# Scores of the first two batches as 64 by 64 corner matmuls, with q stored without zero blocks

## The chip, the cores and the metric

The kernel runs on one core of a Trainium2 chip. Five engines work side by side, each through its own queue in order: TensorE (PE; its weight loads are listed apart as PEld), VectorE (DVE), ScalarE (ACT), GpSimd (POOL) and SyncE (SP), which here only issues DMA transfers. The metric is the device time of one execution in microseconds (us); the median of several runs is compared.

## The reference

Windowed attention over 8 batches, 8 heads, 576 tokens and a head dimension of 64, followed by a feed-forward block with a low-rank mix over tokens. Four heads see a plain window of 32 tokens, four a dilated one.

```python
scores = scale * np.matmul(q, k.transpose(0, 1, 3, 2))
mask_plain = (rel >= 0) & (rel < window)                                   # window = 32
mask_dil = (rel >= 0) & (rel < window * dilation) & (rel % dilation == 0)  # dilation = 4
scores = np.where(masks[None, :, :, :], scores, -1000000000.0)
attn = np.exp(scores - np.max(scores, axis=-1, keepdims=True))
attn = attn / (np.sum(attn, axis=-1, keepdims=True) + 1e-09)
x = np.matmul(attn, v)                 # heads side by side: 576 x 512 a batch
u = x + (x.transpose(0, 2, 1) @ U @ V).transpose(0, 2, 1)
out = u + np.maximum(u @ w_ch1, 0.0) @ w_ch2
```

## The kernel before

**Units and groups.** Tokens of the dilated heads are put in another order by the host, so that their window too is 32 neighbouring tokens. A unit is a pair of heads and a block of 64 queries (`QB`); it needs 96 keys (`KB`: the block and the 32 ahead of it). Four units form a group, nine groups a batch. For a unit the host stores q and k transposed, both heads one above the other on 128 partitions (64 numbers a head). In batches 0 and 1 q of head 0 has its own 64 columns and zeros in the other 64, and q of head 1 the reverse, so that a single float32 matmul of 128 rows by 128 columns against the 96 columns of k gives the scores of both heads, 128 queries by 96 keys (line 388). That makes a row of `QK1` = 128 + 96 = 224 numbers.

**Three ways to load and score.** In batch 0 (groups 0 to 8) `load_qk` brings a whole group at once (line 304), and nine such loads, each followed by a load of v (line 313), are the first things on SP's queue; the loads of the masks, the identity, and then U (`ut`), V (`vt`) and the feed-forward weights come between and behind. In batch 1 `fetch` brings two units at a time (line 336). From batch 2 on, eight of the nine groups of a batch are wide: two neighbouring query blocks of one head fill the 128 columns, without zeros, and the score matmul is that of line 377 on operands split into a high and a low part. The ninth group (`ODD`, the fifth of a batch) has no partner block and stays in the form of batches 0 and 1: four units a batch, one load each (line 342), 24 units in all.

**After the scores.** VectorE adds the mask and takes the minimum of the scaled scores (lines 405 and 408), ScalarE takes the exponential (line 412), the result is transposed by TensorE (line 425) or VectorE (lines 438 and 441), and line 451 multiplies with v: two matmuls a unit, one for each head, each in one half of the array's columns. VectorE divides by the sums (lines 455, 456, 481). The low-rank mix follows (lines 499 to 547).

**The feed-forward block.** Twelve chunks of 384 tokens. For each of the 16 blocks of hidden features `layer1` runs 12 matmuls (line 766), ScalarE and VectorE split the result (lines 771 and 772), and `layer2` runs 9 matmuls into three accumulators (line 786). The weights are loaded as 64-bit floats and narrowed on the chip (lines 201 to 226) during batch 0 and chunk 0.

**What sets the order.** Batch 0 comes first, with the weights' steps put between. Then the chunks run, and `slot` takes attention work of the batches ahead from a list that is sorted by due times, some after every fourth matmul of line 766 and after every third of line 786. So the attention of batch 1 lies in chunk 0 (four units at a time, `step = UNITS`), and from batch 2 on `STEP` = 1: a unit's scores stand alone between feed-forward matmuls. A scheduler then settles each engine's order of instructions by a simulated timeline.

Of the kernel before, what the change touches and what calls it, by code (L numbers as in the profile page):

```python
# [26 lines left out]
P = 128  # L27
QB = 64
NJ = S // QB
KB = QB + WIN  # L30
# [8 lines left out]
CTOK = CT * P  # L39
NCHUNK = NTILE // CT  # L40
UNITS = 4
QK1 = P + KB
DV = D + 1
PV = 2 * DV
KW = P + WIN
# [69 lines left out]
def mask_of(off, n):  # L115
    i = np.arange(n)[:, None]
    c = np.arange(n + WIN)[None, :] - WIN
    ok = (i - c >= 0) & (i - c < WIN)
    if off is not None:
        ok &= (i >= off) == (c >= off)  # L120
    return np.where(ok, 0.0, NEG).astype(np.float32)


def token_of(half, s):
    return s if half == 0 else DIL * (s % RES) + s // RES
# [27 lines left out]
def attention_moe_kernel(ctx: ExitStack, tc: tile.TileContext, qk1, qk2, vv, masks, wide, ident, ut, vt, w1, w2, out):  # L153
    nc = tc.nc
# [110 lines left out]
    at = {}  # L265
# [35 lines left out]
    def load_qk(g):  # L301
        if (g, 0) not in loaded:
            t = early.tile([P, UNITS, QK1], F32, tag="qk", name=f"qk{g}", bufs=QKS)
            nc.sync.dma_start(out=t, in_=qk1[g])
# [22 lines left out]
    def is_odd(n):  # L327
        return n // UNITS % NGB == ODD

    def fetch(n):  # L330
        if n >= UNITS * NG or n in raws:
            return
        if n < N2:
            if n % 2 == 0:
                raw = work.tile([P, 2, QK1], F32, tag="qks", name=f"qkr{n}", bufs=TB)
                nc.sync.dma_start(out=raw, in_=qk1[n // UNITS][:, n % UNITS:n % UNITS + 2])
                raws[n] = raw[:, 0]
                raws[n + 1] = raw[:, 1]
        else:
            raw = work.tile([P, QK2], F32, tag="qk", name=f"qkr{n}", bufs=QKB)  # L340
            m = QK1 if is_odd(n) else QK2
            nc.sync.dma_start(out=raw[:, 0:m], in_=qk2[n - N2][:, 0:m])
            raws[n] = raw

    def split_qk(n):
        if n < N2 or n >= UNITS * NG or n in pairs:
            return
        fetch(n)
        raw = raws[n]
        if is_odd(n):  # L350
            return
        t = work.tile([P, QK3], F32R, tag="qks", name=f"qks{n}", bufs=TB)
        nc.scalar.copy(out=t[:, 0:QK2], in_=raw)  # L353
        nc.gpsimd.tensor_tensor(out=t[:, QK2:], in0=raw[:, P:], in1=t[:, P:QK2].bitcast(F32), op=ALU.subtract)  # L354
        lo = slice(D, P)
        eng = nc.vector if Q_DVE else nc.gpsimd
        eng.tensor_tensor(out=t[lo, 0:P], in0=raw[lo, 0:P], in1=t[lo, 0:P].bitcast(F32), op=ALU.subtract)  # L357
        pairs[n] = t
# [6 lines left out]
    def score(g, u):  # L365
        n = UNITS * g + u
        two = n >= N2 and not is_odd(n)
        if u == 0:
            p_sb = work.tile([P, UNITS, KW], F32, tag="p", name=f"p{g}", bufs=2)
            pool, n_ = (early, 3) if g < NGB else (work, 2)  # L370
            nmax = pool.tile([P, UNITS], F32, tag="nmax", name=f"nmax{g}", bufs=n_)
            state[g] = [p_sb, nmax, None]
        if two:
            sp = psum.tile([P, 2 * KW], F32, tag="ps", name=f"s{g}_{u}")
            split_qk(n)
            t = pairs.pop(n)
            nc.tensor.matmul(sp, lhsT=t[:, 0:P], rhs=t[:, P:], start=True, stop=True)  # L377
        else:
            if n >= N2:
                sp = psum.tile([P, 1, KB], F32, tag="ps", name=f"s{g}_{u}")  # L380
            elif u == 0:
                sp = psum.tile([P, UNITS, KB], F32, tag="acc" if g < NGB else "ps", name=f"s{g}", bufs=3)
            else:
                sp = state[g][2]
            if g >= NE:
                fetch(n)
            t = raws[n] if g >= NE else loaded[g, 0][:, u]
            nc.tensor.matmul(sp[:, u % sp.shape[1], :], lhsT=t[:, 0:P], rhs=t[:, P:QK1], start=True, stop=True)  # L388
        state[g][2] = state[g, u] = sp

    def soften(g, u):
# [214 lines left out]
    def batch_items(b):  # L606
# [3 lines left out]
        for s in range(NGB + LAG):  # L610
# [16 lines left out]
            def some(us, g=g):  # L627
                for u in us:
                    score(g, u)
                for u in us:  # L630
                    n = UNITS * g + u
                    if n >= N2:
                        split_qk(n + LOOK)
                        fetch(n + LOOK + DMA_LOOK)
                    elif n >= UNITS * NE and n % 2 and n + 2 * TB - 1 < N2:
                        fetch(n + 2 * TB - 1)
                for u in us:
                    soften(g, u)
# [109 lines left out]
    for c in range(NCHUNK):  # L748
# [59 lines left out]
        for i in range(CT):  # L808
            t = c * CT + i
# [5 lines left out]
def lay_out(q, k, v, U, V, w1, w2):  # L815

    f = np.float32
    qk1 = np.zeros((B, len(TILES), 2, P, QK1), f)
    qk2 = np.zeros((B - SPLIT, NGB, UNITS, P, QK2), f)
    vv = np.ones((B, len(TILES), 2, KB, PV), f)  # L820
    for half in range(2):
        perm = np.array([token_of(half, s) for s in range(S)])
        hs = slice(half * HH, (half + 1) * HH)
        qp = q[:, hs][:, :, perm].reshape(B, 2, 2, S, D)
        kp = np.zeros((B, 2, 2, WIN + S, D), f)
        vp = np.zeros((B, 2, 2, WIN + S, D), f)
        kp[..., WIN:, :] = k[:, hs][:, :, perm].reshape(B, 2, 2, S, D)
        vp[..., WIN:, :] = v[:, hs][:, :, perm].reshape(B, 2, 2, S, D)
        for j in range(NJ):
            at = TILES.index((half, j))  # L830
            ks = slice(QB * j, QB * j + KB)
            for h in range(2):
                hr = slice(h * D, (h + 1) * D)
                qk1[:, at, :, hr, h * QB:(h + 1) * QB] = qp[:, :, h, QB * j:QB * (j + 1)].transpose(0, 1, 3, 2)
                qk1[:, at, :, hr, P:] = kp[:, :, h, ks].transpose(0, 1, 3, 2)
                vv[:, at, :, :, h * DV:h * DV + D] = vp[:, :, h, ks]
        for i in range(NJ // 2):
            g = TILES.index((half, 2 * i)) // 2
            for u in range(UNITS):
                for r in (slice(0, D), slice(D, P)):  # L840
                    qk2[:, g, u, r, :P] = qp[SPLIT:, u // 2, u % 2, P * i:P * (i + 1)].transpose(0, 2, 1)
                    qk2[:, g, u, r, P:] = kp[SPLIT:, u // 2, u % 2, P * i:P * i + KW].transpose(0, 2, 1)
    qk1 = qk1.reshape(B, NGB, UNITS, P, QK1)
    qk2[:, ODD, :, :, :QK1] = qk1[SPLIT:, ODD]
    qk2 = qk2.reshape((B - SPLIT) * NGB * UNITS, P, QK2)
    qk1 = np.ascontiguousarray(qk1[:SPLIT].reshape(SPLIT * NGB, UNITS, P, QK1).transpose(0, 2, 1, 3))
    vv = np.ascontiguousarray(vv.reshape(B * NGB, UNITS, KB, PV).transpose(0, 2, 1, 3))

    masks = np.stack([np.tile(mask_of(off, QB), (2, 1)) for off in MASK_AT], axis=1)
    wide = np.stack([mask_of(off, P) for off in WIDE_AT], axis=1).astype(ml_dtypes.bfloat16)  # L850

    raw = np.int64
    U, V, w1, w2 = (np.ascontiguousarray(x).view(raw) for x in (U, V, w1, w2))
    ut = np.zeros((P, NU, RANK), raw)
    for a in range(4):
        ut[:, a] = U[a * P:(a + 1) * P]
        ut[:, 4 + a] = U[64 + a * P:64 + (a + 1) * P]
    ut[0:64, 8] = U[512:576]
    ut[64:128, 8] = U[0:64]
    perm = np.array([token_of(1, s) for s in range(S)])  # L860
    for p, js in enumerate(DPART):
        ut[:QB * len(js), 9 + p] = U[perm[QB * js[0]:QB * (js[-1] + 1)]]
    vt = np.zeros((4, RANK, P + S), raw)
    vt[:, :, 64:64 + S] = V
    return {
        "qk1": qk1,
        "qk2": qk2,
        "vv": vv,
        "masks": masks,
        "wide": wide,  # L870
        "ident": np.eye(P, dtype=f),
        "ut": ut.reshape(P, NU * RANK),
        "vt": vt.reshape(P, P + S),
        "w1": w1,
        "w2": w2,
    }
# [15 lines left out]
```

## Time and profile before

| what | value |
|---|---|
| median of 3 runs | 1024.16 us (1022.04 to 1024.59) |
| profiled execution | 1024.88 us, its span 1023.1 us |
| granted TensorE clock, mean | 0.980 |
| PE busy | 983.6 us (96%) |
| DVE, ACT, POOL busy | 624.1, 410.0, 327.9 us |
| DMA | 103.34 MB, 101 GB/s over the span |
| matmuls of line 388 | 192 (two for each of 96 units) |

In rows of the profile, `out<-in` names the tiles written and read, `128*128 128x96` gives the rows and columns of the array that a matmul uses and then the shape of its output, and `x8` counts instructions. `s` is the tile of scores, `qk` and `qkr` the loaded q and k, `pv` the result of line 451, `ph` and `acc` those of lines 766 and 786, `raw` a loaded piece of a weight. [...]

### The profile page before, as it was taken

What the parts mean: (1) busy time and instruction counts of PE and PEld (TensorE: products, weight loads), DVE (VectorE), ACT (ScalarE), POOL (GpSimd) and SP (SyncE); (2) the same over time, 40 slices, a digit from 0 to 9 for tenths busy, and PEclk for the clock granted to TensorE, in tenths of its full rate; (3) what the DMA queues carried; (4) which work ended last, traced back from release to release, by engine and by line L of the source; (5) the groups of instructions that cost most, each with busy time, mean ns of one, the idle gap of its engine ahead of it and who ended that gap; (6) DMA issues with size and microseconds to landing.
All of it is one profiled execution on the core that took longest, in us unless ns stands there. A gap on an engine that the chain in (4) does not pass through costs nothing.

```text
span 1023.1 us, 18253 instructions
## 1 busy us (share of the span) xinstructions
PE 983.6 (96%) x5928; PEld 863.6 (84%) x5928; DVE 624.1 (61%) x2149; ACT 410.0 (40%) x985; POOL 327.9 (32%) x520
## 2 busy tenths in 40 slices
PE   7589998999999999999999999999999999999998
PEld 6388776888888889898888888788888888899996
DVE  4878876777368755777557873787647864411211
ACT  5889873343244423445233432434323442111110
POOL 0568863252143421344131621425213431000000
PEclk9679997999999999999999999999999999999999
DMA  9687643243323423333242432434332420500000
GB/s 255 201 271 234 190 136 106 62 134 87 93 81 83 119 73 90 103 109 100 65 111 74 127 87 52 133 81 121 94 80 81 120 63 25 134 1 1 32 1 32
DMA packets 96912, 103.34 MB, mean 101 GB/s; under 512 B 12816, under 2 KB 83536, under 8 KB 96816
## 3 DMA queue, kind: packets, MB, share of 16 engines
q1 hardware_dynamic: 96816, 102.16, 35.4%
q8 instruction: 48, 0.79, 0.3%
q14 instruction: 48, 0.39, 0.1%
HBM read 80.08 MB, written 17.30 MB: 95 GB/s over the span
## 4 chain that ended last, share of the span: by engine, by line
PE 86%; DMA 5%; DVE 3%; ACT 3%; POOL 1%; issue 1%; SPq 1%; DVEq 0%; POOLq 0%; ACTq 0%
PE acc L786 38%; PE ph L766 37%; PE pv L451 3%; PE s L377 3%; PE t L521 2%; PE m L545 1%; DMA raw<-ut 1%; DMA qk<-qk 1%; PE s L388 1%; DMA qkr<-qk 1%; POOL v L219 1%; ACT v L210 1%; ACT sign L211 1%; DMA raw<-w 1%; DMA v<-vv 1%
## 5 line engine op out<-in xcount | busy, mean ns | idle before, releaser
L786 PE MATMUL acc<-w2h,hh 128*128 128x512 f32 x576 | 229.5, 398 | 1.6 <-DVE x L811 1.1
L786 PE MATMUL acc<-w2l,hh 128*128 128x512 f32 x576 | 228.8, 397 | 0.0
L354 POOL TENSOR_TENSOR qks<-qkr,qks 128x160 fp32r<-128x160 f32 x192 | 103.5, 539 | 385.1 <-ACT qks L353 254.3
L772 DVE SCALAR_TENSOR_TENSOR hl<-ph,hh 128x384 fp32r<-128x384 f32 x192 | 106.2, 554 | 180.4 <-ACT hh L771 179.1
L786 PE MATMUL acc<-w2h,hl 128*128 128x512 f32 x576 | 212.5, 399 | 0.0
L771 ACT ACTIVATE hh<-ph 128x384 fp32r<-128x384 f32 x192 | 93.4, 487 | 268.7 <-PE ph L766 244.1
L766 PE MATMUL ph<-uth,w1l 128*128 128x384 f32 x768 | 175.1, 340 | 0.0
L766 PE MATMUL ph<-utl,w1h 128*128 128x384 f32 x768 | 173.0, 339 | 1.2 <-DVE utl L604 1.2
L766 PE MATMUL ph<-uth,w1h 128*128 128x384 f32 x768 | 172.5, 340 | 0.6 <-ACT uth L603 0.3
L412 ACT ACTIVATE p<-p,nmax 128x160 f32<-128x160 f32 (+1 forms) x288 | 111.0, 408 | 123.5 <-DVE nmax L408 122.5
L766 PEld LDWEIGHTS ph<-uth,w1h 128*128 128x128 f32 x768 | 138.6, 189 | 17.1 <-ACT uth L603 1.7
L766 PEld LDWEIGHTS ph<-utl,w1h 128*128 128x128 f32 x768 | 135.0, 188 | 2.9 <-DVE utl L604 1.6
L766 PEld LDWEIGHTS ph<-uth,w1l 128*128 128x128 f32 x768 | 136.2, 189 | 1.1 <-issue 0.4
L353 ACT CAST qks<-qkr 128x288 fp32r<-128x288 f32 x192 | 80.7, 429 | 125.1 <-PE s L377 92.8
L786 PEld LDWEIGHTS acc<-w2h,hl 128*128 128x128 f32 x576 | 107.7, 189 | 23.8 <-issue 0.4
L786 PEld LDWEIGHTS acc<-w2h,hh 128*128 128x128 f32 x576 | 108.5, 188 | 18.5 <-ACT hh L771 2.2
L786 PEld LDWEIGHTS acc<-w2l,hh 128*128 128x128 f32 x576 | 108.5, 188 | 15.9
L438 DVE STREAM_TRANSPOSE pt<-p 32x128 f32<-32x128 f32 x384 | 115.7, 301 | 10.1 <-ACT p L412 5.1
L405 DVE TENSOR_TENSOR p<-s,wide_sb 128x160 f32<-128x160 f32 x192 | 60.2, 319 | 74.1 <-PE s L377 72.3
L357 POOL TENSOR_TENSOR qks<-qkr,qks 64x128 fp32r<-64x128 f32 x192 | 90.6, 472 | 15.1
L501 POOL TENSOR_TENSOR xhl<-x,xhl 128x256 fp32r<-128x256 f32 (+1 forms) x68 | 50.1, 758 | 80.3 <-ACT xhl L499 48.9
L377 PE MATMUL s<-qks 128*128 128x320 f32 x192 | 60.8, 325 | 1.7 <-DVE x L547 1.7
(75 smaller groups left out, 977.2 us busy)
## 6 DMA issues: line engine op xcount, KB each, us to landing
qkr<-qk SPq DMA_DIRECT2D x192, 144.0 KB, 2.2
raw<-w SPq DMA_DIRECT2D x26, 512.0 KB, 5.0
v<-vv SPq DMA_DIRECT2D x126, 97.5 KB, 2.1
out<-x SPq DMA_DIRECT2D x36, 256.0 KB, 2.2
zd<-z SPq DMA_DIRECT2D x120, 64.0 KB, 2.0
xt<-zd SPq DMA_DIRECT2D x30, 256.0 KB, 2.9
qk<-qk SPq DMA_DIRECT2D x9, 448.0 KB, 9.4
qkr<-qk SPq DMA_DIRECT2D x18, 224.0 KB, 4.4
```

What stands on the lines that cost most here:

```text
L353: nc.scalar.copy(out=t[:, 0:QK2], in_=raw)
L354: nc.gpsimd.tensor_tensor(out=t[:, QK2:], in0=raw[:, P:], in1=t[:, P:QK2].bitcast(F32), op=ALU.subtract)
L357: eng.tensor_tensor(out=t[lo, 0:P], in0=raw[lo, 0:P], in1=t[lo, 0:P].bitcast(F32), op=ALU.subtract)
L377: nc.tensor.matmul(sp, lhsT=t[:, 0:P], rhs=t[:, P:], start=True, stop=True)
L405: nc.vector.tensor_tensor(out=p_sb[:, u, :], in0=sp[:, 0:KW], in1=wide_sb[:, kind], op=ALU.add)
L412: nc.scalar.activation(out=p_sb[:, u, 0:w], in_=p_sb[:, u, 0:w], func=AF.Exp, bias=nmax[:, u:u + 1], scale=-1.0,)
L438: nc.vector.transpose(out=to[:, :, WIN * (r % 2):WIN * (r % 2 + 1)], in_=p_sb[rs, :, QB * s + WIN * k:QB * s + WIN * (k + 1)])
L501: eng.tensor_tensor(out=xl[rs], in0=x[rs], in1=xh[rs].bitcast(F32), op=ALU.subtract)
L766: nc.tensor.matmul(ph, lhsT=w[:, k, :], rhs=u[:, k, :], start=(n == 0), stop=(n == len(seq) - 1))
L771: nc.scalar.activation(out=hh, in_=ph, func=AF.Relu)
L772: nc.vector.scalar_tensor_tensor(out=hl, in0=ph, scalar=0.0, in1=hh.bitcast(F32), op0=ALU.max, op1=ALU.subtract)
L786: nc.tensor.matmul(acc[i], lhsT=h[:, ss], rhs=w, start=(c > 0 and f == 0 and n == 0), stop=(f == FC - 1 and n == 2))
```

## The change

The zero blocks go. Both heads' q stand in the same 64 columns, head 0 on the first 64 partitions, head 1 on the others, so a unit's row has `QK1` = 64 + 96 = 160 numbers. The score matmul of line 388 becomes two, one a head: 64 rows by 64 columns, head 0 in the first corner of the array (rows 0 to 63, columns 0 to 63), head 1 in the opposite one (64 to 127 each), each giving 64 queries by 96 keys in its half of the same output tile. This holds for batches 0 and 1 and for the odd group of the later ones. Wide groups stay as they are.

```diff
-QK1 = P + KB
+QK1 = QB + KB
...
             t = raws[n] if g >= NE else loaded[g, 0][:, u]
-            nc.tensor.matmul(sp[:, u % sp.shape[1], :], lhsT=t[:, 0:P], rhs=t[:, P:QK1], start=True, stop=True)
+            for h in range(2):
+                hr = slice(QB * h, QB * (h + 1))
+                nc.tensor.matmul(sp[hr, u % sp.shape[1], :], lhsT=t[hr, 0:QB], rhs=t[hr, QB:QK1], start=True, stop=True)
...
             for h in range(2):
                 hr = slice(h * D, (h + 1) * D)
-                qk1[:, at, :, hr, h * QB:(h + 1) * QB] = qp[:, :, h, QB * j:QB * (j + 1)].transpose(0, 1, 3, 2)
-                qk1[:, at, :, hr, P:] = kp[:, :, h, ks].transpose(0, 1, 3, 2)
+                qk1[:, at, :, hr, 0:QB] = qp[:, :, h, QB * j:QB * (j + 1)].transpose(0, 1, 3, 2)
+                qk1[:, at, :, hr, QB:] = kp[:, :, h, ks].transpose(0, 1, 3, 2)
```

## The prediction

> **What bounds the kernel now.** I read the head of the page first, then its slices, then busy time by stretch, then the chain of work that ended last, and only then single matmuls in the timeline.
>
> ```profile
> span 1023.1 us, 18253 instructions
> PE 983.6 (96%) x5928; PEld 863.6 (84%) x5928; DVE 624.1 (61%) x2149; ACT 410.0 (40%) x985; POOL 327.9 (32%) x520
> ...
> PE   7589998999999999999999999999999999999998
> ...
> DMA  9687643243323423333242432434332420500000
> ```
>
> TensorE (PE) is full from the third slice on; the DMA engines are full only in the first. So a microsecond of TensorE work saved or added late moves the end by about as much, and at the start the loads decide. Busy time by stretch is sharper (columns: stretch, its length, busy time of PE, PEld, DVE, ACT and POOL with their instructions, granted clock, DMA share, GB/s):
>
> ```profile
> 10.00:15.00 5.00, 5.00 (x44) 4.64 (x41) 2.61 (x21) 3.28 (x10) 0.00 (x0) 1.00 1.05 265
> 15.00:20.00 5.00, 3.72 (x46) 3.07 (x45) 3.57 (x25) 2.91 (x10) 0.00 (x0) 1.00 1.06 267
> 20.00:25.00 5.00, 4.61 (x70) 3.93 (x69) 4.55 (x31) 3.80 (x11) 0.00 (x0) 1.00 1.04 263
> 35.00:55.00 20.00, 10.55 (x73) 7.16 (x73) 18.33 (x38) 15.21 (x32) 15.52 (x13) 0.50 0.54 166
> 60.00:100.00 40.00, 38.42 (x268) 34.48 (x268) 31.98 (x94) 38.12 (x78) 33.73 (x25) 0.95 0.80 251
> 100.00:145.00 45.00, 41.08 (x285) 34.86 (x285) 34.38 (x100) 37.64 (x94) 36.45 (x33) 1.00 0.59 180
> 200.00:877.00 677.00, 674.57 (x4093) 593.63 (x4093) 448.73 (x1612) 256.06 (x633) 220.42 (x412) 1.00 0.34 91
> ```
>
> From 10 to 25 us the DMA share is 1.04 to 1.06 at about 265 GB/s: loads bind. From 35 to 55 us VectorE (DVE) does, 18.33 of 20. From 60 to 145 us four engines are nearly full together. From 200 us it is TensorE alone, 674.57 of 677. The chain agrees for the start (columns: start, length, what), where one transfer waits for another:
>
> ```profile
> 3.06 5.72 DMA v<-vv
> ...
> 8.80 9.40 DMA qk<-qk
> ...
> 18.22 10.03 DMA raw<-ut
> ```
>
> **The loads.** Their number and their place on SP's queue stay; a unit's row goes from 224 to 160 numbers, so each load has 5/7 of its bytes (columns: engine, operation, count, KB of one, us to landing):
>
> ```profile
> qk<-qk SPq DMA_DIRECT2D x9, 448.0 KB, 9.4
> qkr<-qk SPq DMA_DIRECT2D x18, 224.0 KB, 4.4
> ...
> qkr<-qk SPq DMA_DIRECT2D x24, 112.0 KB, 2.0
> v<-vv SPq DMA_DIRECT2D x9, 195.0 KB, 8.5
> ```
>
> In batch 0 a group of four units needs 448 + 195 = 643 KB, 2.48 us at 265 GB/s; it will need 320 + 195 = 515 KB, 1.99 us. Over nine groups the loads alone give 9 x 0.49 = 4.4 us, and that is the upper end. VectorE comes next: 3.57 + 4.55 us in the 10 us from 15 to 25, four groups, so 2.0 us a group, and 2.25 in the second half alone. I take 2.1 us as the new pace: 9 x (2.48 - 2.1) = 3.4 us earlier, for the attention of batch 0 and for the load of ut behind it, from which the chain goes on through ScalarE and VectorE. The lower end is 0: from 35 to 55 us VectorE has 18.33 of 20 us, and if it works there on what came in early anyway, the first feed-forward matmul does not move. I take 3.4, as the chain goes through the load of ut. The 18 loads of batch 1 lose 18 x 64 KB = 1.2 MB while DMA is at 0.80 and four engines are busier; I cost that at nothing, since those engines hide it, and so for the 24 loads after 190 us (share 0.34).
>
> **The score matmuls.** A float32 matmul is two weight loads and two matmuls in the trace. The odd groups of the six late batches score one unit at a time, 24 units in all, amid full-array matmuls (columns: start, busy time, engine, line, shapes, count):
>
> ```profile
> 196.97 0.39 PE L786 MATMUL acc<-w2l,hh 128*128 128x512 f32 x1
> 197.20 0.40 PE L786 MATMUL acc<-w2h,hl 128*128 128x512 f32 x1
> 197.44 0.36 PE L388 MATMUL s<-qkr 128*128 128x96 f32 x2
> 197.58 0.48 PE L786 MATMUL acc<-w2h,hh 128*128 128x512 f32 x1
> 197.90 0.39 PE L786 MATMUL acc<-w2l,hh 128*128 128x512 f32 x1
> ```
>
> L786 to L786 is 0.23 us. From the unit's start to the second L786 behind it is 0.46, so the unit costs 0.46 - 0.23 = 0.23 us. After the change it is four loads and four matmuls in two corners of 64 by 64. The nearest row is line 521 at 64*64:
>
> ```profile
> 150.04 0.39 PE L786 MATMUL acc<-w2l,hh 128*128 128x512 f32 x1
> 150.27 0.64 PE L786 MATMUL acc<-w2h,hl 128*128 128x512 f32 x2
> 150.83 0.33 PE L521 MATMUL t<-xhl,us 64*64 64x256 f32 x1
> 151.09 0.50 PE L786 MATMUL acc<-w2h,hl 128*128 128x512 f32 x1
> 151.43 0.33 PE L766 MATMUL ph<-uth,w1h 128*128 128x384 f32 x1
> ```
>
> Three L786 take 0.79 us here instead of 0.69: going into a part of the array costs 0.10. From L521 to the second full matmul is 0.60, less one L786 0.37: 0.26 from L521 to the first one and 0.11 more behind it, as that one is busy 0.50 instead of 0.39: its weights were not loaded ahead. What several small matmuls cost inside the part I take from the attention's second matmul, line 451, in two column halves:
>
> ```profile
> 88.72 0.40 PE L786 MATMUL acc<-w2l,hh 128*128 128x512 f32 x1
> 89.05 0.69 PE L451 MATMUL pv<-v,pt 96*64 96x65 f32 x16
> 89.66 1.13 PE L388 MATMUL s<-qkr 128*128 128x96 f32 x8
> 90.63 0.60 PE L425 MATMUL ptp<-id_sb,p 128*96 128x128 f32 x4
> ...
> L451 PE MATMUL pv<-v,pt x1152: 220/222/370, 13.2 to 851.7; 96*64 96x65 f32 x192
> ```
>
> Sixteen take 0.69, of which 0.22 is the last one's own duration (the last row's median, 222 ns), so 0.47 / 8 = 0.058 us for a pair: both halves run side by side. Two pairs with the way back are 0.61 - 6 x 0.058 = 0.26 us. An odd unit will cost 0.10 + 0.26 + 0.11 = 0.47, so 0.24 more than now. Not all 24 pay that:
>
> ```profile
> 203.87 0.35 PE L388 MATMUL s<-qkr 128*128 128x96 f32 x2
> 204.16 0.69 PE L451 MATMUL pv<-v,pt 96*64 96x65 f32 x16
> ...
> 437.34 0.58 PE L388 MATMUL s<-qkr 128*128 128x96 f32 x4
> ```
>
> Six units stand beside an L451 burst, where a change of the array's parts is paid already (an estimate of 0.06 more each), and four stand in two pairs like 437.34 (0.13 more a pair). The sum is 14 x 0.24 + 6 x 0.06 + 2 x 0.13 = 4.0 us, all on the path, as nothing but TensorE binds there. Ends: 24 x 0.06 = 1.4, were all beside bursts, and 24 x 0.24 = 5.8.
>
> In batch 1 four units are scored together behind L451. The eight matmuls at 89.66 take 0.97 us to the next line. In corners they are 16, like the burst at 89.05: 0.61, and about 0.09 for longer rows and the next line's bare weight load, 0.70. So 0.27 us less a group, 2.4 over nine. But only part lies on the chain:
>
> ```profile
> 81.85 1.06 PE s L388 x8
> ...
> 89.73 1.06 PE s L388 x8
> ```
>
> Four groups stand in the chain between 60 and 100 us; later ones lie beside POOL's and ACT's weight preparation (36.45 and 37.64 of 45). I take 4 x 0.27 = 1.1, ends 0 and 2.4. Batch 0's scores stand under its loads: nothing. DVE, ACT and POOL get no work more or less, and no wait is added: line 408 on VectorE still waits for a unit's last score matmul, which comes about 0.1 us later in an odd unit, under other work of an engine with 448.73 of 677 us.
>
> Sum: -3.4 - 1.1 + 4.0 = -0.5 us. The profiled execution took 1024.88 us, 0.7 above the median of 1024.16; on the median that is 1023.7.
>
> **Rivals.**
> 1. *The start's gain is swallowed.* VectorE at 18.33 of 20, or the weight preparation up to 145 us, sets the pace whatever the loads do. For it: four full engines there; against it: the chain hangs on the load of ut until 28 us. Then -1.1 + 4.0 = +2.9, 1027.1, and slower as soon as the odd units cost 4.2 instead of 4.0 or batch 1 gives 0.9 instead of 1.1: an even chance.
> 2. *The clock steps.* The granted clock falls by halves where TensorE pauses:
>
> ```profile
> 70.00:75.00 5.00, 5.00 (x21) 4.02 (x22) 4.86 (x19) 5.00 (x12) 4.58 (x4) 0.66 0.99 297
> ...
> 160.00:170.00 10.00, 5.06 (x19) 3.53 (x18) 8.12 (x24) 4.48 (x11) 3.92 (x8) 0.66 0.66 189
> ```
>
>    At 70 us a third of 5 full microseconds is lost, 1.7; at 160 us about 0.34 x 10, of which TensorE was there for half, so some 2. Loads that come earlier may remove the pauses ahead: -0.5 - 1.7 - 2 = -4.2, 1020.0. They may as well add one.
> 3. *The corners go in turn.* No row shows two row halves side by side, only column halves. Then a single unit costs 0.06 more (24 x 0.06 = 1.4) and a group 16 x 0.058 + 0.15 = 1.08 against 0.97, so +0.4 instead of -1.1: -3.4 + 0.4 + 5.4 = +2.4, 1026.6. Both heads' scores go to one tile in PSUM, on different partitions. [...]
> 4. *No change of parts is paid.* If the corners run as the full array does, four loads of half the columns cost what two did, in odd units and in groups: -3.4 alone, 1020.8. The rows at 150.83 speak against it.
>
> **How the numbers follow.** My sum 0.48, the start swallowed 0.17, the clock 0.18, in turn 0.10, no change of parts 0.07. About 0.3% (3.1 us) is what a measurement of this kernel tells from no change: faster is under 1021.1, slower over 1027.2. Faster: 0.17 of the clock, 0.07 of the fourth, 0.05 of my own with start and batch 1 at their ends; 0.29. Slower: half of the first rival (0.085), almost half of the third (0.045), 0.05 of my own; 0.18. The rest, 0.53, is no change. The range goes from 1019.0 (a little beyond the second rival) to 1028.5 (the first with odd units at their upper end). My own case alone is 1021.5 to 1026.
>
> **What would show it.** The load of ut lands near 24.5 us instead of 28.25, and the first L766 is some 3 us earlier; if only the first comes true, the first rival holds. Line 388's successor has 384 matmuls of 64*64; a pair's starts lie a few ns apart or, in turn, some 58. From 200 us on, the same chunks of work take about 4 us longer in all, with L786 or L766 behind a unit of scores starting late. PEclk at 70 and 160 us decides the second. I would be wrong most likely through an order of instructions on TensorE that comes out otherwise: more units beside bursts, or fewer.

## The result and the profile after

The changed kernel takes 1030.35 us (median of 6 runs, 1029.45 to 1033.21) against 1024.38 of the kernel before, measured beside it: a ratio of 1.0066, 95% interval 1.0049 to 1.0083. It is 6 us slower, above the upper end of the range. One of the six runs of the kernel before took 1364.08 us; the ratio leaves it out. The profiled execution took 1029.58 us. First the head of the page and one row of its DMA issues (line numbers from 390 on are two higher than before):

```profile
span 1027.8 us, 18646 instructions
PE 989.1 (96%) x6120; PEld 858.3 (84%) x6120; DVE 625.3 (61%) x2149; ACT 408.1 (40%) x985; POOL 327.6 (32%) x520
...
PE   4779998999999999999999999999999999999998
...
DMA  9668444243232433333242432424332320500000
...
qk<-qk SPq DMA_DIRECT2D x9, 320.0 KB, 7.0
```

The loads shrank as planned, 448 to 320 KB, and land after 7.0 us instead of 9.4. Nevertheless the first slice of TensorE fell from 7 to 4 tenths, although nothing was taken from it but waiting for loads. The same stretches as in the prediction (length, busy time of PE, PEld, DVE, ACT and POOL, granted clock, DMA share, GB/s) show the place:

```profile
10.00:15.00 5.00, 4.98 (x67) 3.56 (x65) 2.50 (x24) 4.28 (x15) 0.00 (x0) 1.00 1.06 280
15.00:20.00 5.00, 3.66 (x72) 3.02 (x70) 3.15 (x17) 0.51 (x2) 0.00 (x0) 1.00 1.06 269
20.00:25.00 5.00, 0.00 (x0) 0.00 (x0) 0.00 (x0) 0.43 (x1) 0.00 (x0) 0.64 1.03 336
...
60.00:100.00 40.00, 35.79 (x273) 31.12 (x275) 37.11 (x88) 36.09 (x74) 32.24 (x24) 0.84 0.75 236
100.00:145.00 45.00, 44.45 (x352) 38.10 (x346) 32.80 (x106) 33.50 (x88) 28.56 (x25) 1.00 0.49 151
200.00:877.00 677.00, 676.12 (x4127) 588.85 (x4127) 448.32 (x1619) 253.66 (x632) 220.24 (x412) 1.00 0.33 90
```

From 20 to 25 us TensorE and VectorE do nothing and ScalarE 0.43 us; before, they had 4.61, 4.55 and 3.80. The granted clock falls to 0.64 in the same stretch. The chain of waits there, and the waits between 14 and 31 us (engine, line, what it waited for, sum, count, longest):

```profile
15.86 8.69 DMA raw<-ut
24.55 0.02 issue
24.57 0.60 ACT v L210
```

```profile
POOL v L219 <- ACT sign L212: 25.9, 2, 24.7
ACT v L210 <- DMA raw<-ut: 9.1, 1, 9.1
PEld ptp L427 <- ACT p L414: 8.3, 2, 8.1
DVE v L218 <- ACT v L210: 8.1, 3, 6.9
PE ptp L427 <- ACT p L414: 7.9, 1, 7.9
```

ut landed at 24.55 instead of 28.25 us, as forecast. But ScalarE had been waiting for it since 15.5 us: its queue now has the narrowing of ut (lines 210 to 212) after 16 exponentials, four groups; in the kernel before it stood after 31, nearly eight groups. The exponentials of the fifth group are behind it, the transposes (line 427) wait for those, and everything stands. The same waits before:

```profile
ACT v L210 <- DMA raw<-ut: 2.3, 1, 2.3
ACT pt L427 <- PE ptp L425: 2.2, 3, 1.2
```

By the timelines the last multiplication with v of the fourth group of batch 0 ends at 31.6 instead of 23.0, that of the ninth at 54.5 instead of 42.4. The first feed-forward matmul starts at 74.0 instead of 62.3. This 12 us delay shrinks on the way, as TensorE is fuller from 100 to 145 us (44.45 against 41.08). Ends of the chunks of the feed-forward block, by the additions that close them, in us:

| end of chunk | 0 | 1 | 2 | 3 | 4 | 5 | 6 | 7 | 8 | 9 | 11 |
|---|---|---|---|---|---|---|---|---|---|---|---|
| before | 161.7 | 257.2 | 334.1 | 413.0 | 493.5 | 570.3 | 653.2 | 732.9 | 809.8 | 887.6 | 1019.5 |
| after | 166.3 | 260.6 | 338.6 | 417.0 | 498.2 | 575.7 | 656.8 | 737.4 | 815.0 | 892.4 | 1024.2 |
| difference | 4.6 | 3.4 | 4.5 | 4.0 | 4.7 | 5.4 | 3.6 | 4.5 | 5.2 | 4.8 | 4.7 |

Of the 4.7 us between the two traces, one execution each, 4.6 are there when chunk 0 ends. Later the loss goes up and down by about one.

### The profile page after: what moved, and what is told of

Same layout as the page of the kernel before. It is cut to its first block, busy times and chain, and to the rows that moved or that the text cites. A ratio compares the mean times of both kernels' runs of the same rounds, so it can differ in the third digit from the quotient of the medians.

```text
span 1027.8 us, 18646 instructions
## 1 busy us (share of the span) xinstructions
PE 989.1 (96%) x6120; PEld 858.3 (84%) x6120; DVE 625.3 (61%) x2149; ACT 408.1 (40%) x985; POOL 327.6 (32%) x520
## 4 chain that ended last, share of the span: by engine, by line
PE 86%; ACT 5%; DVE 4%; DMA 3%; issue 1%; POOL 1%; SPq 0%; DVEq 0%; ACTq 0%; POOLq 0%
PE acc L788 38%; PE ph L768 37%; PE pv L453 4%; PE s L377 3%; PE t L523 2%; ACT sign L211 1%; PE m L547 1%; ACT p L414 1%; PE s L390 1%; ACT v L210 1%; ACT sign L212 1%; DMA zd<-z 1%; DMA raw<-ut 1%; DMA qk<-qk 1%; DVE v L218 1%
```

## The experiments

Each time stands beside runs of the kernel before on the same chip (1022.95 to 1024.10 in the five sets). Theory: what ScalarE's queue does in batch 0. Rivals: the corners themselves, the loads, the order in chunk 0.

**One part alone.** First the narrowing was to be held back in the changed kernel. For ut and the three pieces behind it GpSimd copies four numbers a partition from a later group's probabilities into the tile that the narrowing writes; `PRE_AT` puts these steps four places later in the program, behind the groups that they now need.

```diff
-PRE_AT = range(1, 7)
+PRE_AT = range(5, 11)
+PIN = {0: 6, 1: 7, 2: 7, 3: 8}
...
+            if i - 1 in PIN:
+                nc.gpsimd.tensor_copy(out=v[:, 0:UNITS], in_=probs[PIN[i - 1]][:, :, 0])
```

> The changed kernel, with the narrowing of ut, vt and the first weight made to wait (through four numbers that GpSimd copies from the probabilities of groups 6, 7, 7 and 8), so that ScalarE has the exponentials of seven groups ahead of ut, not of four. Order theory: what was lost is ScalarE's wait of 9.1 us for ut with five groups' exponentials behind it; the first feed-forward matmul comes from 74.0 us back to 62 or below, chunk 0 ends at 160 or below instead of 164.4, and the time falls by 4 us or more, to 1026 or less. Switch theory: the loss is what 24 odd units pay for going into corners and back, about 4.8 us, and a late start is made up in chunk 0; the start moves, the time stays within 1 us of 1030.

Measured: 1027.58, ratio 1.0044 (1.0028 to 1.0059). Neither forecast holds it, and the waits between 14 and 31 us say why:

```profile
POOL v L288 <- ACT p L419: 28.4, 1, 28.4
ACT sign L212 <- DMA raw<-ut: 8.4, 1, 8.4
```

The narrowing of a piece has three steps; the copy held the first, and the second (here line 212, into another tile) still stood in front of the fifth group. The wait moved by a line and stayed 8.4 us. So this run alone decides nothing.

Next, the odd groups of the late batches get their zero blocks and the full matmul back:

```diff
+            if n >= N2:
+                nc.tensor.matmul(sp[:, 0, :], lhsT=t[:, 0:P], rhs=t[:, P:QKO], start=True, stop=True)
+            else:
...
```

> The changed kernel, but the odd groups of batches 2 to 7 keep zero blocks and one matmul of the full array. Switch theory: 24 x 0.2 = 4.8 us less, near 1025.5. Order theory: the start is as bad as in the changed kernel (first feed-forward matmul near 74 us); the time falls only by what the odd units cost in the stretch that TensorE binds, 1 to 2 us by the ends of the chunks, near 1029.

1027.71, ratio 1.0029 (1.0014 to 1.0044), some 2.6 us less than the changed kernel and between the two forecasts. Chunk 0 still ends at 166.0, ScalarE waits 7.6 us for ut: the start's loss is not the odd units'.

The loads alone: compact storage, but the full matmul on it, which adds the scores of both heads (its attention is another function; work and shapes are those of the kernel before).

```diff
-            for h in range(2):
-                hr = slice(QB * h, QB * (h + 1))
-                nc.tensor.matmul(sp[hr, u % sp.shape[1], :], lhsT=t[hr, 0:QB], rhs=t[hr, QB:QK1], start=True, stop=True)
+            nc.tensor.matmul(sp[:, u % sp.shape[1], :], lhsT=t[:, 0:P], rhs=t[:, QB:QK1], start=True, stop=True)
```

> The compact data, but one matmul of 128 rows by 128 columns for each unit as before (its columns are the 64 of q and the first 64 of k, so the two heads' scores are added up and are not told apart); no corners. Order theory: ScalarE has ut after six groups, two more than with corners, so it waits some 4 us and the first feed-forward matmul comes between 60 and 68 us; 1020 to 1026. Switch theory: no corners, so the 3.4 us of the loads alone remain, 1021.

1019.72, ratio 0.9956 (0.994 to 0.9971): 4.4 us faster. Chunk 0 ends at 158.4, 3.3 earlier than before. Here the narrowing came after six groups and ScalarE's wait was short:

```profile
ACT v L210 <- DMA raw<-ut: 2.9, 1, 2.9
```

And the corners alone, on the old storage:

```diff
+            for h in range(2):
+                hr = slice(QB * h, QB * (h + 1))
+                nc.tensor.matmul(sp[hr, u % sp.shape[1], :], lhsT=t[hr, QB * h:QB * (h + 1)], rhs=t[hr, P:QK1], start=True, stop=True)
```

> The storage with zero blocks as before, but two corner matmuls a unit. Order theory: ScalarE has ut after five groups, while ut lands as late as before (28.3 us), so it waits some 9 us or more, the first feed-forward matmul comes at 72 us or later, and the time is 1029 to 1033. Switch theory: 4.8 us for the odd units less 1.1 in batch 1, 1028.

1025.86, ratio 1.0018 (1.0004 to 1.0032), below both forecasts. Chunk 0 ends at 165.1, 3.4 us later than before, and the wait is back, with no change of any load. Chunk 1 gives 3.6 us back (91.9 instead of 95.5), as it has none of the 10.2 us at half clock that the kernel before has from 163.2 us.

```profile
ACT v L210 <- DMA raw<-ut: 6.5, 1, 6.5
```

So the wait comes with the corners: the three kernels that have them in batch 0 and nothing held back (this one, the changed kernel, the one with odd groups restored) wait 6.5 to 9.1 us, those with full matmuls (the kernel before and the loads alone) 2.3 and 2.9. The scheduler places the narrowing by its own simulated times, and more matmuls in batch 0 changed where it fell. That the higher count of matmuls is the reason is argued, not shown.

**The wait taken away, and put in.** The same hold, with two copies more for each of the four pieces, into the tiles of the other two steps:

```diff
+                for w in range(2):
+                    nc.gpsimd.tensor_copy(out=signs[i % NSIGN][:, 0:UNITS, w], in_=early_p)
```

> Like the kernel of the first experiment, but the two other narrowing steps of ut (lines 211 and 212), which had stayed ahead of the fifth group's exponentials there and kept ScalarE waiting 8.4 us, are made to wait as well. Order theory: ScalarE has seven groups ahead of ut and waits under 2 us; the first feed-forward matmul comes at 62 us or earlier and the time is that of the loads alone (1019.7) plus what odd units cost, 1021 to 1023. Rival (the corners cost the time by themselves, in batches 0 and 1 and in odd units): the time stays at 1027 or above.

1017.87, ratio 0.9944 (0.9927 to 0.9961). Against the hold of one step that is 9.7 us, for eight small copies. It is also less than the 1021 to 1023 expected, so the wait may not be all of it: up to the end of chunk 0 only 174 of ScalarE's 276 instructions keep their order between these two runs. Its waits (no row of ScalarE for ut is left) and its stretches:

```profile
POOL v L289 <- ACT p L422: 23.0, 2, 22.9
ACT p L422 <- DVE nmax L418: 3.2, 3, 2.3
```

```profile
15.00:20.00 5.00, 5.00 (x80) 3.70 (x78) 4.64 (x26) 2.66 (x10) 0.00 (x0) 1.00 1.07 282
20.00:25.00 5.00, 4.85 (x84) 3.73 (x85) 4.71 (x30) 3.82 (x12) 0.41 (x3) 1.00 1.03 338
```

TensorE has 4.85 of the 5 us in which it had none, chunk 0 ends at 150.7 instead of 164.6. A clock step then takes some of it back: chunk 1 lasts 99.4 instead of 94.6, with 13.7 us at half clock from 153.1 (6.8 there).

The converse came last: the kernel before, with neither corners nor compact storage, gets the wait.

```diff
+        if g == 4 and u == 0:
+            nc.gpsimd.tensor_copy(out=p_sb[:, :, 0], in_=pipe[0][1][:, 0:UNITS])
         for rs, w, a, c in todo:
```

> The kernel before, old storage and full score matmuls, with one copy of four numbers on GpSimd from the narrowed ut into the fifth group's tile of probabilities, ahead of that group's mask step: the narrowing of ut (and of both halves of vt, by the order that comes out) now stands ahead of the fifth group's exponentials on ScalarE, as ut's does in the changed kernel. Theory (a load waited for by ScalarE in the middle of batch 0 is what lost the time): ScalarE waits some 9 us for ut, TensorE and VectorE stand still from about 19 to 28 us, the fourth to ninth groups of batch 0 end 10 to 14 us later than in the kernel before, the first feed-forward matmul starts at 72 to 76 instead of 62.3, the first chunk ends 4 to 9 us later, and the time is 1028 to 1034. Rival (the wait is only a neighbour of the loss; the time went to the corners and to the order in the first chunk): the wait appears but the first chunk ends within 2 us of 161.7, and the time is 1022 to 1026.

1031.83, ratio 1.0088 (1.0068 to 1.0107). The waits and the stretches:

```profile
ACT v L210 <- DMA raw<-ut: 6.8, 1, 6.8
```

```profile
20.00:25.00 5.00, 1.40 (x24) 1.17 (x22) 2.63 (x10) 0.00 (x0) 0.00 (x0) 0.97 1.05 286
25.00:30.00 5.00, 0.00 (x0) 0.00 (x0) 1.63 (x3) 3.64 (x9) 1.48 (x2) 0.50 1.06 339
```

TensorE stands still from 25 to 30 us, the first feed-forward matmul starts at 74.8 (74.0 in the changed kernel) and chunk 0 ends at 172.6, further out than the 4 to 9 us expected. Here the narrowing of both halves of vt stands in front as well. So a standstill of this kind suffices for a loss of this size, with no corner and no compact load. The copy also makes the fifth group depend on ut by its data, so this run prices the standstill, not the order of the queue alone.

**The parts without the wait.** The same full hold on the kernel before, then on the changed kernel with the odd groups restored:

> The kernel before with the same made-up waits, whose order on ScalarE is then the one that it had but for vt. Both theories: within 2 us of 1024; it says what the waits cost by themselves.

> The kernel of the previous experiment but one (all three narrowing steps of ut wait), and the odd groups keep zero blocks and one full-array matmul. Both theories: the difference to that kernel is the odd units' corners alone. By the single units' rows (0.28 us more for each of 14, less beside bursts) 4 us; by the ends of the chunks, where waits in chunks 3, 6 and 9 shrink in exchange, 1 to 2 us. Order theory: 1019 to 1021.

1014.76, ratio 0.992 (0.9902 to 0.9939), and 1014.29, ratio 0.9911 (0.9893 to 0.9928). They beat the kernel before by 8.8 and 9.3 us, where the first was expected within 2 us of 1024. Under one hold, on one chip, the parts read: odd units 1017.87 - 1014.29 = 3.6 us; loads and corners of batches 0 and 1 together 1014.29 - 1014.76 = -0.5. So 3.1 of the 6 us between the two kernels are left under the hold. In the pair for the odd units VectorE, ScalarE and GpSimd keep their whole order up to the end of chunk 0; its traces are 2.1 us apart at the end of chunk 1, where the half clock lasts 13.7 instead of 10.2, and 3.9 at the end of chunk 11. The kernel with loads and corners ends chunk 0 2.7 us earlier (151.0 against 153.7) and loses it in chunk 1 (97.0 against 93.7): the half clock around 155 us lasts 10.2 instead of 6.8. That the kernel before gains 9 us although its own wait was 2.3 is more than this wait explains; the hold also changes other orders, and in its trace ut landed at 25.26, 3.0 us earlier with the same loads. How much each is worth stays open.

To see the start without corners and without zeros in HBM, batch 0's q went compact into tiles that GpSimd had zeroed, k in loads of its own:

```diff
+                nc.gpsimd.memset(q[0:D, :, QB:], 0.0)
+                nc.gpsimd.memset(q[D:, :, 0:QB], 0.0)
...
+                    nc.sync.dma_start(out=q[hr, :, h * QB:(h + 1) * QB], in_=q0[hr, g * UNITS:(g + n) * UNITS])
```

> The kernel before, but in batch 0 q comes without zero blocks into tiles whose zero blocks GpSimd sets at the start, and k by itself; one full-array matmul a unit everywhere, so no corners. Loads of the first groups have 5/7 of the bytes, in six loads more. Order theory: ScalarE has ut ahead of the sixth group's last exponential (23 of 36 done) and waits 2 to 4 us; 1019 to 1024. Rival (the loads alone decide): 1020.

1024.12, ratio 1.0006 (0.9993 to 1.0018): no gain. It was a poor test, since one big load of q for four groups made the second group late (its last multiplication with v ended at 24.6).

Loads alone and corners alone under the hold, each as above on the held kernel before:

> The kernel of the third experiment (compact data, one full-array matmul a unit that adds the two heads' scores up) with the made-up waits. Against the kernel before with the same waits (1014.8) it has 5/7 of the bytes in the loads and nothing else. If loads still bind once ScalarE's order is mended: 3 to 4 us less, 1011 to 1012. If not (kernel e7 got 0.5 us from loads and corners in batches 0 and 1 together, as its chunk 0 ended 2.7 us earlier and chunk 1 took 3.3 us longer): 1014 to 1015.

> The kernel of the fourth experiment (zero blocks stored as before, two corner matmuls a unit) with the made-up waits. Against the kernel before with the same waits (1014.8) it has the corners and nothing else. By the two pinned kernels that differ in the odd units alone, 3.6 us more for those, less up to 1.1 for batch 1: 1017 to 1019. If corners cost the start something that is no order of ScalarE's: above 1020.

1017.79, ratio 0.9941 (0.9922 to 0.9961), and 1027.39, ratio 1.0028 (1.0016 to 1.004). By ratios against 0.992, loads now cost 2 us and corners 11, while the whole change cost 3.1 under the hold (1017.87 against 1014.76). Both forecasts for the loads failed, and by the condition set for the corners (above 1020) they cost the start something that is no order of ScalarE's. But the hold settles only the narrowing. Up to the end of chunk 0 ScalarE keeps the order of the held kernel before in 152 of 276 instructions with the loads, 218 with the corners and 179 with both and the odd groups restored. So these differences are not prices of loads or corners. With the corners chunk 0 ends at 161.2 instead of 153.7, with half clock from 31.1 to 58.4 us; ScalarE waits 1.9 us for ut there, no single wait explains the loss, and it stays open.

**An order that is not settled by simulated times.** All four with the scheduler's simulated timeline off, so that instructions keep more of the program's order:

```diff
-    with tile.TileContext(nc, schedule_with_timeline_sim=True) as tc:
+    with tile.TileContext(nc, schedule_with_timeline_sim=False) as tc:
```

> The kernel before without the scheduler's simulated timeline, so that every engine's instructions stand nearly in the order of the program text. No time is forecast for it alone; it is the base of the next three.

> The changed kernel without the simulated timeline. Its order agrees with that of the run above in 952 of 987 instructions on ScalarE and 2112 of 2151 on VectorE (with the timeline only 768 and 1339 agree between the kernels before and after). Order theory: at a held order the change is worth what the prediction's sum said, -0.5 us against the run above, between -3 and +2. Rival (loads or corners cost the time by themselves): +6 as between the two kernels that are compared here.

> The changed kernel without the simulated timeline, odd groups with zero blocks and one full-array matmul. All compute engines have the order of the run above, so the difference is the odd units alone: by their rows 4 to 5 us less; if waits elsewhere take it in, 1 to 2 us less.

> The compact data with one full-array matmul a unit (which adds the two heads' scores up), without the simulated timeline. Against the first of these four: the loads alone, by the prediction 3.4 us less, ends 0 and 4.4; 959 of 987 and 2102 of 2151 instructions stand in the same order.

| kernel, plain order | median, us | ratio (interval) | end of chunk 0 |
|---|---|---|---|
| before | 1107.8 | 1.0821 (1.0805 to 1.0837) | 234.1 |
| after | 1101.37 | 1.0757 (1.0737 to 1.0776) | 220.6 |
| after, odd groups restored | 1091.28 | 1.0665 (1.0642 to 1.0687) | 218.5 |
| loads alone | 1093.67 | 1.068 (1.0664 to 1.0696) | 221.2 |

In none of these four does ScalarE wait for ut. At a nearly held order the change is 6.4 us faster (952 of ScalarE's 987 instructions stand in the same order, against 768 in the delivered pair). The loads alone give 14.1, all by the end of chunk 0; the half clock after 114 us lasts 75 us in all before and 55 with them. The odd units cost 10.1, with all other compute engines in identical order: 2.1 in chunk 0, which has no odd unit, and 4.0 in chunk 5, where a wait of TensorE has different lengths. All three differences lie outside their forecasts. After, in plain order, TensorE's waits from 590 to 606 us and the stretch of them:

```profile
PE s L377 <- DVE x L483: 2.2, 1, 2.2
```

```profile
594.00:614.00 20.00, 17.83 (x109) 15.24 (x108) 14.54 (x59) 7.59 (x20) 7.55 (x16) 0.91 0.33 92
```

With the odd groups restored, from 586 to 600 us:

```profile
PE s L378 <- DVE x L487: 1.0, 1, 1.0
```

After the wait of 2.2 us the clock stood at half for 3.4 us (0.91 over the 20), after the one of 1.0 it did not fall. That is no threshold, for in the run of the loads alone a longer wait, which ends at 352.2 us, is followed by no lower clock (its waits from 345 to 356 us and the stretch behind):

```profile
PE s L377 <- DVE x L481: 2.4, 1, 2.4
```

```profile
352.00:356.00 4.00, 3.77 (x19) 3.27 (x19) 3.36 (x17) 2.16 (x6) 1.62 (x4) 1.00 0.25 75
```

Four units' own cost in that chunk is about 1 us, so 3 of the 4.0 are wait and clock. Without these and the 2.1 of chunk 0 some 5 us are left for the odd units, between the prediction's 4.0 and its upper end of 5.8.

## Why the prediction was wrong

**The step that failed** is "DVE, ACT and POOL get no work more or less, and no wait is added", on which "I take 3.4, as the chain goes through the load of ut" rests. The work is the same; the order of ScalarE's queue is not, and it adds a wait of 9.1 us. I warned of an order that comes out otherwise, but on TensorE alone. The row that could have warned was in the trace of before: ScalarE already waited 2.3 us for ut (28.28 us in the chain), so the narrowing stood before the load's arrival with the end of group eight behind it, and each group fewer ahead of it would lengthen the wait by about the pace of a group (an estimate from my 2.1 us). That such a wait costs time is shown by putting it in (8.9 us slower than the kernel before beside it) and by taking it away (9.7 us, though other orders changed with it); and in plain order, where nothing on ScalarE waits for ut, the change is 6.4 us faster. What share of the 6 us it has is not shown: under the hold the changed kernel is still 3.1 us behind. ScalarE kept its order through that wait: VectorE had the minima of the fifth group ready at 18.4 us, but its exponentials started at 26.2, behind the three steps of ut that began at 24.57 (the row "ACT v L210 <- DMA raw<-ut: 9.1").

**Loads, -3.4.** ut landed at 24.55 (forecast 24.5), which is in part luck: over all profiled kernels with the same order of loads it landed at 26.6 on average with the old storage and at 24.6 with the compact one, 2.0 us apart and not 3.7. Alone the loads gave 4.4 us in the scheduler's order; in plain order 14.1, and under the hold they cost 2. A range of 0 to 4.4 was too narrow for a term that depends on the order.

**Batch 1's scores, -1.1.** The gain of a group is smaller than 0.27. In the timeline of after:

```profile
91.17 0.69 PE L453 MATMUL pv<-v,pt 96*64 96x65 f32 x16
91.78 0.88 PE L390 MATMUL s<-qkr 64*64 64x96 f32 x16
92.59 0.64 PE L427 MATMUL ptp<-id_sb,p 128*96 128x128 f32 x4
```

From line 390 to the next 0.81 us instead of 0.97: 0.16 a group, or 0.6 us for the four groups. Eight of these matmuls elsewhere (two odd units side by side) take 0.55:

```profile
322.64 0.55 PE L390 MATMUL s<-qkr 64*64 64x96 f32 x8
```

So a pair of corners follows the last by (0.88 - 0.55) / 4 = 0.08 us, where I had taken 0.058 from the column halves of line 451. Those give 65 columns of output and these 96; in proportion, an estimate, 0.058 x 96 / 65 is 0.086.

**Batch 0's scores, "under its loads: nothing".** True of their time, not of their effect: with them the narrowing moved.

**Odd units, +4.0.** Right in size for a unit, but "all on the path" was wrong. A single unit in the timeline of after, and line 390's durations (min, median, max in ns, first and last start):

```profile
205.61 0.40 PE L788 MATMUL acc<-w2h,hl 128*128 128x512 f32 x1
205.94 0.38 PE L390 MATMUL s<-qkr 64*64 64x96 f32 x4
206.25 0.50 PE L788 MATMUL acc<-w2h,hh 128*128 128x512 f32 x1
206.59 0.40 PE L788 MATMUL acc<-w2l,hh 128*128 128x512 f32 x1
...
L390 PE MATMUL s<-qkr x240: 242/243/346, 72.5 to 805.7; 64*64 64x96 f32 x120
```

From 205.61 to 206.59 is 0.98, less two steps of 0.23: the unit costs 0.52, 0.28 more than the 0.24 that the same reckoning gives at 197.44 us before; the forecast was 0.24 more. The way in is 0.10 (0.33 instead of 0.23), as forecast from line 521. The late start behind is there too: line 788 at 206.25 is busy 0.50 instead of 0.40, and the next starts 0.34 behind it, 0.11 more than 0.23, as forecast. The odd units stand in chunks 1, 2, 4, 5, 7 and 8, four in each. Chunks 2, 4, 5, 7 and 8 grew by 1.1, 0.7, 0.7, 0.9 and 0.7, 4.1 us for 20 units, so 0.2 each. But chunks 3, 6 and 9 shrank by 0.5, 1.8 and 0.4, so that chunks 2 to 9 are only 1.4 us longer, not "about 4". Of these 2.7 us of gain TensorE's waits between 257 and 900 us give 1.7, first before, then after:

```profile
PE ph L766 <- DVE utl L604: 1.2, 1, 1.2
PE acc L786 <- DVE x L811: 1.1, 1, 1.1
PE ph L766 <- ACT uth L603: 0.3, 1, 0.3
```

```profile
PE acc L788 <- DVE x L813: 0.9, 1, 0.9
```

**The rivals.** The first, the start's gain swallowed, is nearest in outcome (1027.1) but named VectorE and the weights' preparation, not ScalarE's queue. In the second the clock did step otherwise, but to no gain: the 10.2 us at half clock around 168 us became 6.8, while the half clock ahead of 75 us grew from 30.7 us in all to 47.8, behind the standstill at 20 us. The third, corners in turn, falls: four matmuls of a unit in 0.38 us, of which 0.24 is the last one's own, leave 0.14 for the starts, and the two opposite corners of a pair start 7 ns apart (6 or 7 in 160 of the 192 pairs). Both write one tile, on different partitions, and go side by side. The fourth falls by the 0.10 us on the way in.

## What to carry to other kernels

Where a scheduler settles the order, the cost of an edit is its instructions plus whatever the order does: here ScalarE's wait of 9.1 us for ut held up the fifth group's exponentials, which stood behind it. List on each engine what stands behind each step that waits for a late load, before and after. In the two runs that took such a wait away or put it in, about 9 us hung on it, more than on any instruction changed. Price an edit with the order held, and see that it is held on every engine; then look for a hold on the order itself: a dozen small copies gained more than the change was to give, and the best version is the kernel before with the narrowing held back (1014.76) or the changed one with the odd groups restored as well (1014.29).

## What the runs showed of the hardware

The same loads in the same queue order moved at different rates. The stretch from 10 to 15 us of the held kernel before, whose loads are those of the kernel before (265 GB/s there):

```profile
10.00:15.00 5.00, 5.00 (x43) 4.55 (x42) 2.23 (x16) 2.93 (x10) 0.00 (x0) 1.00 1.04 310
```

In six profiled kernels with old storage, with the same 22 loads in the same order on SP's queue, ut landed at 25.2 to 28.3 us; in ten with compact storage at 23.7 to 25.8. In all sixteen SyncE issued ut 0.02 us after the eighth load before it had landed, so no compute engine set this pace. So the same bytes spread over 3 us, nearly my whole term, at a DMA share of 1.04 to 1.06 from 10 to 25 us, which went with 263 to 267 GB/s in the kernel before and with 306 to 328 in the held one: 265 GB/s from one profile was no safe price.

Opposite corners of the array that write one tile ran side by side (a pair's starts 7 ns apart, above), and the four small matmuls of the unit at 205.94 us cost 0.52 us where the burst at 91.78 has 0.08 from pair to pair: by estimate 0.52 - 2 x 0.08 = 0.36 was the way in and out, most of it.
